# Fourier attention with routed experts: GpSimd splits the experts' weights alone, the bias is copied one mixing ahead, and batch 1's first stage begins inside batch 0

## The chip, the cores and the metric

One core of one Trainium2 chip runs the whole program. The metric is the device time of one execution in microseconds (us); of several runs the median is given. The core's compute engines run side by side, each in its own instruction order: TensorE (PE, its weight loads are listed apart as PEld), VectorE (DVE), ScalarE (ACT) and GpSimd (POOL). SyncE (SP) issues the transfers between the chip's memory and the core, in order too.

## What is computed

The reference takes 8 sequences of 2496 tokens with 256 numbers each through a Fourier mixing, and its result through a layer of 8 experts, of which each token uses one:

```python
X = np.fft.rfft(x, axis=1)
Yr = Xr @ w_r - Xi @ w_i + b_r
Yi = Xr @ w_i + Xi @ w_r + b_i
Yr = sign(Yr) * maximum(abs(Yr) - 0.01, 0);  Yi = sign(Yi) * maximum(abs(Yi) - 0.01, 0)
y = np.fft.irfft(Yr + 1j * Yi, n=2496, axis=1)

logits = y @ w_gate + modality_bias[modality_id]        # 19968 tokens, 8 experts
e_idx = argmax(logits);  gate = softmax(logits)[e_idx]
out = gate * (maximum(y @ w1[e_idx], 0) @ w2[e_idx])     # 256 -> 1024 -> 256
```

## The kernel before

**Attention.** The Fourier transform of 2496 points is done as 39 times 64 points, both stages as matrix products. Per batch `b` there are four pieces of work.

- The first stage has 11 chunks `c` (`s1_load`, `s1_split`, `s1_chunk`). A chunk's input `x` is split into a rounded part `x1h` and a rest `x1l` (L250, L251); three products (L266 to L268) go into one PSUM tile; ACT copies it into half of an `ev` buffer (L271); when an `ev` buffer is full, SP stores it to the scratch `scr` in memory (L275). There are three `ev` buffers. In batch 0 two of them are borrowed, at pair 3, for constants (`tri_st` L411 and `st_g` L206) until pair 6.
- The second stage goes over 10 pairs `p` of frequencies. `a_load` brings a pair from `scr` (L283), `s2_pair` transforms it (L292) and splits it into `Xh` and `Xl` (ACT L297 and L299, DVE L298 and L300). `mix_bias` has ACT copy the bias into a PSUM tile `mx` (L309), and `mix_sums` adds 24 products to it (L329). `shrink` makes `u` (ACT L337) and `s` (DVE L338) of it, and `is2_pair` begins the way back (L353, copied to `z` at L356). `mx` has two PSUM tiles.
- The second inverse stage has 22 pivots `j` (L369, ACT L374, DVE L375), each followed by three products into `i` (L381 to L383). Between them lie the first-stage chunks of batch `b + 2`; in batch 0 the chunks of batch 1 lie among the pairs instead.
- Routing is on DVE and GpSimd; GpSimd scatters the rows of a finished batch to their experts' places with indirect transfers (L537), four after each pair from 6 on and the rest among the pivots.

**Splitting the weights.** Through the attention, `SplitWeights` takes the experts' weights apart in 64 pieces of 128 by 512. `step` has ACT cast a loaded piece `wr` to `wh` (L978), then GpSimd or DVE subtract to get `wl` (L979); SP stores both to `wsp` (L980, L981) and loads the next piece (L963). `wh` and `wl` have one buffer each, `wr` two. The steps that lie among the pairs use GpSimd (47), those among the pivots DVE (17).

**Experts.** 78 tiles of 256 tokens (and a few half tiles) are taken through the split weights (L804 to L847).

**What sets the order.** PE, ACT, DVE and GpSimd run in an order that a scheduler fixes from the order of the code in `build`. SP issues in order too, and the number of its transfers in flight is limited, so that a transfer that has to wait holds up those behind it. `issue_after` puts transfers into SP's row behind a given one.

Of the kernel before, what the change touches and what calls it, by code (L numbers as in the profile page):

```python
# [9 lines left out]
F32 = mybir.dt.float32  # L10
# [130 lines left out]
class Attn:  # L141
# [112 lines left out]
    def s1_chunk(self, b, c, ahead):  # L254

        nc = self.nc
        u, h = c // 2, c % 2
        xh, xl = self.xs.pop((b, c))
        if h == 0:
            if u == 0 :  # L260
                self.scr[b] = self.dr.tile([2 * K1, N2P, D], F32, tag="scr", name=f"scr_{b}")
            self.ev = self.w3.tile([128, 4 * D], F32, tag="ev", name=f"ev_{b}_{u}")[:PK].rearrange("p (j d) -> p j d", d=D)

        pool, tag = (self.rps, "r") if b == 1 or c < 2 else (self.ps, "x" if b and c < 9 else "y")
        ps = pool.tile([128, 512], F32, tag=tag, name=f"s1_{b}_{c}")
        nc.tensor.matmul(ps[:PK], self.f[:, 0, :PK], xh, start=True, stop=False)  # L266
        nc.tensor.matmul(ps[:PK], self.f[:, 1, :PK], xh, start=False, stop=False)
        nc.tensor.matmul(ps[:PK], self.f[:, 0, :PK], xl, start=False, stop=True)  # L268
        if ahead and c + ahead < 11:
            self.s1_split(b, c + ahead)  # L270
        nc.scalar.copy(self.ev[:, 2 * h:2 * h + 2, :].rearrange("p j d -> p (j d)"), ps[:PK])  # L271
        if h == 1 or c == 10:
            n = min(4, J - 4 * u)
            rows = self.scr[b].rearrange("k (g j) d -> (k g) j d", g=3)
            self.stored = nc.sync.dma_start(rows[:, 4 * u:4 * u + n, :], self.ev[:, :n, :])  # L275
# [672 lines left out]
class SplitWeights:  # L948
# [17 lines left out]
            self.nc.sync.dma_start(raw.rearrange("p (c d) -> p c d", d=D), src[:, (c - 4) * 2:(c - 4) * 2 + 2, :])  # L966
        self.raw.append((e, c, raw))

    def step(self, eng):
        if not self.raw:  # L970
            return
        nc = self.nc
        e, c, raw = self.raw.pop(0)
        hi = self.one.tile([128, 512], F32R, tag="wh", name=f"wh_{e}_{c}")
        lo = self.one.tile([128, 512], F32R, tag="wl", name=f"wl_{e}_{c}")
        row = self.wsp[e * 128:(e + 1) * 128, :]
        o = c * 512 if c < 4 else 4096 + (c - 4) * 512
        nc.scalar.copy(hi, raw)  # L978
        eng.tensor_sub(lo, raw, hi)  # L979
        nc.sync.dma_start(row[:, o:o + 512], hi.bitcast(F32))  # L980
        nc.sync.dma_start(row[:, o + 2048:o + 2560], lo.bitcast(F32))  # L981
        self.load()


def build(tc, I, out, nb):
    nc = tc.nc
    with ExitStack() as outer:
        dp = outer.enter_context(tc.tile_pool(name="wsp", bufs=1, space=DRAM))
        wsp = dp.tile([E * 128, 8192], F32, name="wsp")
        with ExitStack() as ctx:  # L990
# [39 lines left out]
            at.consts_first()  # L1030
            for u, v in ((0, 1), (1, 2), (2, 5)):
                at.s1_load(0, u, v)
            ins = at.s1_load(0, 5)
            with tc.issue_after(ins.ins):
                mixing = at.consts_mix()
                next(mixing, None)
                at.table_load("m", 0)
            at.s1_split(0, 0)
            at.s1_split(0, 1)
            for c in range(11):  # L1040
                at.s1_chunk(0, c, 2)
            with tc.issue_after(at.stored.ins):
                at.s1_load(1, 0)
                ins = load(0)
            with tc.issue_after(ins.ins):
                load(1)
                at.s1_load(1, 1)
                load(2)
                at.table_load("q", 0)
                ins = at.s1_load(1, 2)  # L1050
            next(mixing, None)
            bias(0)
            at.s1_split(1, 0)
            at.s1_split(1, 1)
            at.s1_chunk(1, 0, 2)
            s2(0)
            at.s1_chunk(1, 1, 2)
            s2(1)
            mix(0)
            bias(1)  # L1060
            with tc.issue_after(ins.ins):
                ins = load(3)

# [2 lines left out]
            for b in range(nb):  # L1066
                done = b == nb - 1
                for p in range(10):
# [4 lines left out]
                    if b == 0:  # L1073
                        with tc.issue_after(ins.ins):
                            if p % 2 == 0 and p < 8:
                                at.table_load("m", p // 2 + 1)
                                at.table_load("q", p // 2 + 1)
                            ins = load(i + 4)
                        with tc.issue_after(ins.ins):
                            if p < 3:  # L1080
                                at.s1_load(1, p + 3)
                            if p == 3 or p > 4:
                                at.s1_load(2, max(p - 4, 0))
                            if p == 2:
                                sw.load()
                                sw.load()
                        s2(i + 2)
                        if p == 3:
                            late = [rt.consts(), at.consts_last()]
                        if p in (3, 6):  # L1090
                            for g in late:
                                next(g, None)
                        for c in ((2,), (3, 4), (5, 6), (7, 8), (9, 10))[p] if p < 5 else ():
                            at.s1_chunk(1, c, 2)
                    else:
                        if p > 0:
                            ins = load(i + 4) or ins
                            s2(i + 2)
                        u = {1: 0, 2: 1, 3: 2, 4: 3, 7: 4, 9: 5}.get(p)
                        if u is not None and b + 2 < nb:  # L1100
                            with tc.issue_after(ins.ins):
                                at.s1_load(b + 2, u)
                    if p < 6 if b > 0 else 2 < p < 8:
                        sw.step(nc.gpsimd)
                    if p > 5:
                        rt.scatter(4)
                    if done and 4 < p < 9:
                        bias(i + 2)
                    ending = i == last - 2
                    if ending:  # L1110
                        mix_last(i + 1, 0)
                    else:
                        mix(i + 1, 0 if apart else None)
                    if p < 9 and not (done and p > 4):
                        bias(i + 2)
                    if due:
                        state = next(routing, None)
                    at.is2_pair(b, p, ss.pop(i))
# [20 lines left out]
                for j in range(J):  # L1139
                    rt.scatter(1)  # L1140
                    pend.append((j, at.pivot(b, j)))
                    chunk = j % 2 == 1 and j != 15
                    if len(s1) > 4 and chunk:
                        at.s1_split(*s1[4])
                    if len(pend) > 2:
                        jj, r = pend.pop(0)
                        at.is1(b, jj, *r, nc.scalar.copy if done or jj % 2 else nc.vector.tensor_copy)
                    if j in (8, 18) or (b == 0 and j == 13) or (b == nb - 2 and j in (3, 13)):
                        sw.step(nc.vector)
                    if s1 and chunk:  # L1150
                        at.s1_chunk(*s1.pop(0), 0)
                    next(routing, None)
# [9 lines left out]
                    routing = chain(routing, rt.tiles_early())  # L1162
                if b == nb - 2:
                    rt.fence()
        with ExitStack() as ctx:
            ctx.enter_context(tc.manual_schedule(engines={ET.PE, ET.Activation, ET.DVE, ET.Pool}))
            ex = Experts(ctx, tc, I, out, rt, wsp)
# [36 lines left out]
```

## Time and profile before

| what | us |
|---|---|
| median of 3 runs (lowest, highest) | 1618.44 (1617.22, 1621.98) |
| the profiled execution: its own time | 1625.38 |
| its span, from the first instruction to the last | 1623.6 |
| busy in it: PE, PEld | 1529.5, 1486.9 |
| busy in it: DVE, ACT, POOL | 693.2, 655.9, 561.0 |
| first product of the experts | 709.64 |

The profile is of one execution. Busy time is what an engine spends in instructions, without the waits. A wait is named by who waited (engine, tile, line) and by what came last before it went on. "PEclk" is the share of its full clock that TensorE was granted. Rows of the DMA queue are those that SP issued; their second number is the time from one issue to the next, and not how long a transfer takes.

### The profile page before, as it was taken

What the parts mean: (1) busy time and instruction counts of PE and PEld (TensorE: products, weight loads), DVE (VectorE), ACT (ScalarE), POOL (GpSimd) and SP (SyncE); (2) the same over time, 40 slices, a digit from 0 to 9 for tenths busy, and PEclk for the clock granted to TensorE, in tenths of its full rate; (3) what the DMA queues carried; (4) which work ended last, traced back from release to release, by engine and by line L of the source; (5) the groups of instructions that cost most, each with busy time, mean ns of one, the idle gap of its engine ahead of it and who ended that gap; (6) DMA issues with size and microseconds to landing.
All of it is one profiled execution on the core that took longest, in us unless ns stands there. A gap on an engine that the chain in (4) does not pass through costs nothing. (4 is left out here: it accounts for less than half of the span.)

```text
span 1623.6 us, 34686 instructions
## 1 busy us (share of the span) xinstructions
PE 1529.5 (94%) x12459; PEld 1486.9 (92%) x12459; DVE 693.2 (43%) x1452; ACT 655.9 (40%) x1345; POOL 561.0 (35%) x548
## 2 busy tenths in 40 slices
PE   5899899989999969799999999999999999899998
PEld 3889898989898959699999999999999999899998
DVE  4455565556565536244333333333333333233332
ACT  3466665556665526242232233223322323232332
POOL 0121727272736341512552223222322222222332
PEclk7999999999999979889999999999999999999999
DMA  8777676767675635632343422752224227634541
GB/s 270 236 212 249 206 233 199 227 199 234 197 245 169 212 93 182 200 125 48 80 131 61 152 43 53 251 154 44 53 52 147 42 53 251 212 86 145 157 122 53
DMA packets 289103, 246.68 MB, mean 152 GB/s; under 512 B 207168, under 2 KB 242388, under 8 KB 285217
## 3 DMA queue, kind: packets, MB, share of 16 engines
q1 hardware_dynamic: 269937, 202.85, 43.8%
q0 software_dynamic: 18992, 41.58, 7.7%
q8 instruction: 100, 1.64, 0.4%
q14 instruction: 74, 0.61, 0.1%
HBM read 434.30 MB, written 100.73 MB: 330 GB/s over the span
## 5 line engine op out<-in xcount | busy, mean ns | idle before, releaser
L834 PE MATMUL y<-w,hh 128*128 128x256 f32 x2496 | 436.4, 278 | 0.0
L804 PE MATMUL h<-xh,w 128*128 128x256 f32 x2496 | 404.3, 279 | 5.4 <-DMA w<-wsp 5.4
L834 PEld LDWEIGHTS y<-w,hh 128*128 128x128 f32 x2496 | 378.2, 188 | 0.8
L834 PE MATMUL y<-w,hl 128*128 128x256 f32 x1248 | 347.8, 279 | 0.3 <-DVE hl L807 0.2
L804 PEld LDWEIGHTS h<-xh,w 128*128 128x128 f32 x2496 | 340.4, 189 | 5.9 <-issue 5.0
L807 DVE SCALAR_TENSOR_TENSOR hl<-h,hh 128x512 fp32r<-128x512 f32 x312 | 209.4, 689 | 234.2 <-ACT hh L806 186.5
L847 POOL DMA_INDIRECT out<-o,ix x161 | 158.4, 984 | 429.7 <-ACT o L826 392.1
L804 PE MATMUL h<-xl,w 128*128 128x256 f32 x1248 | 245.6, 278 | 0.0
L806 ACT ACTIVATE hh<-h 128x512 fp32r<-128x512 f32 x312 | 178.2, 595 | 158.1 <-PE h L804 142.2
L834 PEld LDWEIGHTS y<-w,hl 128*128 128x128 f32 x1248 | 234.2, 188 | 1.5 <-DVE hl L807 1.1
L329 PE MATMUL mx<-wmix,Xh 128*128 128x256 f32 x1280 | 188.8, 291 | 21.6 <-ACT mx L309 16.7
L329 PEld LDWEIGHTS mx<-wmix,Xh 128*128 128x128 f32 x1280 | 166.6, 195 | 29.5 <-ACT mx L309 21.3
L804 PEld LDWEIGHTS h<-xl,w 128*128 128x128 f32 x1248 | 189.8, 189 | 0.0
L826 ACT ACTIVATE o<-y,xt 128x256 f32<-128x256 f32 x78 | 37.0, 475 | 344.9 <-PE y L834 344.9
L784 POOL TENSOR_TENSOR xl<-tr,xh 128x512 fp32r<-128x512 f32 x78 | 101.0, 1295 | 210.1 <-ACT xh L783 209.3
L824 DVE TENSOR_SCALAR o<-y,xt 128x256 f32<-128x256 f32 x78 | 37.8, 484 | 316.2 <-ACT o L826 311.9
L979 POOL TENSOR_TENSOR wl<-wr,wh 128x512 fp32r<-128x512 f32 x47 | 60.0, 1277 | 277.1 <-ACT wh L978 199.0
L375 DVE TENSOR_TENSOR pl<-pv,ph 120x264 fp32r<-120x264 f32 x176 | 75.3, 431 | 100.1 <-ACT ph L374 63.3
L338 DVE SCALAR_TENSOR_TENSOR s<-mx,u 128x512 f32<-128x512 f32 (+1 forms) x81 | 55.5, 685 | 143.2 <-ACT u L337 123.7
L369 PE MATMUL pv<-pv,z 128*120 128x136 f32 x704 | 114.4, 289 | 2.1 <-ACT z L356 2.1
L369 PEld LDWEIGHTS pv<-pv,z 128*120 128x120 f32 x704 | 102.2, 191 | 9.9 <-ACT z L356 4.1
L329 PE MATMUL mx<-wmix,Xl 128*128 128x256 f32 x640 | 102.9, 284 | 1.1 <-issue 0.9
(185 smaller groups left out, 2060.1 us busy)
## 6 DMA issues: line engine op xcount, KB each, us to landing
w<-wsp SPq DMA_DIRECT2D x166, 2048.0 KB
a<-scr SPq DMA_DIRECT2D x160, 128.0 KB
xt<-xs SPq DMA_DIRECT2D x624, 32.0 KB
scr<-ev SPq DMA_DIRECT2D x40, 480.0 KB
x<-in_x SPq DMA_DIRECT2D x37, 512.0 KB
wr<-in_moe_w SPq DMA_DIRECT2D x64, 256.0 KB
wsp<-wh SPq DMA_DIRECT2D x64, 256.0 KB
wsp<-wl SPq DMA_DIRECT2D x64, 256.0 KB
```

The costliest lines, as they stand in the source:

```text
L329: self.nc.tensor.matmul(ps[i][:, i, :], t[:, 2 * i + c, o:o + 128], self.w[:, wi, c, lo, :], start=False, stop=n == len(ops) - 1, skip_gro ...
L338: nc.vector.scalar_tensor_tensor(s, ps, LAM, u, ALU.add, ALU.min)
L369: nc.tensor.matmul(ps[:PK, c * 128:c * 128 + D // 2 + E], self.z[:, o:o + 3, :, :].rearrange("p n k r -> p (n k r)"), self.pv[:, c, :], st ...
L375: nc.vector.tensor_sub(pl, ps[:PK, :GC], ph)
L784: nc.gpsimd.tensor_sub(xl, tr, xh)
L804: nc.tensor.matmul(ps[:, q, :], w1[:, lo, c, f * 128:(f + 1) * 128], x[:, c, :], start=n == 0, stop=n == 5)
L806: nc.scalar.activation(hh[:, 2 * p:2 * p + 2, :], ps, AF.Relu)
L807: nc.vector.scalar_tensor_tensor(hl[:, 2 * p:2 * p + 2, :], ps, 0.0, hh[:, 2 * p:2 * p + 2, :], ALU.max, ALU.subtract)
L824: nc.vector.tensor_scalar_mul(o[:, s, :], y[s], gate)
L834: nc.tensor.matmul(y[s], lhsT, w2[:, lo, f, :], start=n == 0, stop=n == 23)
L847: ins = self.nc.gpsimd.indirect_dma_start(out=self.out, out_offset=bass.IndirectOffsetOnAxis(ap=ix, axis=0), in_=o, in_offset=None, bounds ...
L979: eng.tensor_sub(lo, raw, hi)
```

## The change

It has three parts.

1. `step` has GpSimd do both the cast (now L982) and the subtraction (now L983), in all 64 steps. ACT loses 64 casts and DVE 17 subtractions. In batch 0 the steps lie at pairs 5 to 9 instead of 3 to 7, and the first two pieces are loaded at pair 3 instead of 2.
2. `bias(i + 2)` stands ahead of `mix(i + 1)`, so ACT copies the bias of the mixing after the next one before it makes the shrink of the next one. `bias(1)` is done before the first mixing.
3. Batch 0's chunks from 6 on write into buffers of the input pool (`wx`, four buffers) instead of `ev`. Two loads of batch 1's input (`x_1_0`, `x_1_1`) go ahead of batch 0's stores, batch 1's chunks 0 to 3 are done before the first pair, and then one chunk each at pairs 0, 1 and 2, instead of one, two and two.

The lines after L258 are shifted by 4 in the changed kernel (L268 becomes L272).

```diff
@@ s1_chunk
-            self.ev = self.w3.tile([128, 4 * D], F32, tag="ev", name=f"ev_{b}_{u}")[:PK].rearrange("p (j d) -> p j d", d=D)
+            if b == 0 and u > 2:
+                ev = self.wx.tile([128, 4, D], F32, tag="x", name=f"ev_{b}_{u}").rearrange("p j d -> p (j d)")
+            else:
+                ev = self.w3.tile([128, 4 * D], F32, tag="ev", name=f"ev_{b}_{u}")
+            self.ev = ev[:PK].rearrange("p (j d) -> p j d", d=D)
@@ SplitWeights
-    def step(self, eng):
+    def step(self):
...
-        nc.scalar.copy(hi, raw)
-        eng.tensor_sub(lo, raw, hi)
+        nc.gpsimd.tensor_copy(hi, raw)
+        nc.gpsimd.tensor_sub(lo, raw, hi)
@@ build, ahead of the pairs
-            ins = at.s1_load(0, 5)
+            at.s1_load(0, 5)
+            ins = at.s1_load(1, 0)
             with tc.issue_after(ins.ins):
                 mixing = at.consts_mix()
                 next(mixing, None)
-                at.table_load("m", 0)
+                ins = at.table_load("m", 0)
+            with tc.issue_after(ins.ins):
+                at.s1_load(1, 1)
...
             with tc.issue_after(at.stored.ins):
-                at.s1_load(1, 0)
                 ins = load(0)
             with tc.issue_after(ins.ins):
-                load(1)
-                at.s1_load(1, 1)
+                ins = load(1)
+            next(mixing, None)
+            at.s1_split(1, 0)
+            at.s1_split(1, 1)
+            for c in range(4):
+                with tc.issue_after(ins.ins):
+                    at.s1_chunk(1, c, 2 if c < 2 else 0)
+            with tc.issue_after(ins.ins):
                 load(2)
                 at.table_load("q", 0)
                 ins = at.s1_load(1, 2)
-            next(mixing, None)
             bias(0)
-            at.s1_split(1, 0)
-            at.s1_split(1, 1)
-            at.s1_chunk(1, 0, 2)
+            bias(1)
             s2(0)
-            at.s1_chunk(1, 1, 2)
             s2(1)
+            at.s1_split(1, 4)
             mix(0)
-            bias(1)
@@ build, the pairs
-                            if p == 2:
+                            if p == 3:
                                 sw.load()
                                 sw.load()
...
-                        for c in ((2,), (3, 4), (5, 6), (7, 8), (9, 10))[p] if p < 5 else ():
-                            at.s1_chunk(1, c, 2)
+                        for c in ((4,), (5,), (6,), (7, 8), (9, 10))[p] if p < 5 else ():
+                            at.s1_chunk(1, c, 1)
...
-                    if p < 6 if b > 0 else 2 < p < 8:
-                        sw.step(nc.gpsimd)
+                    if p < 6 if b > 0 else p > 4:
+                        sw.step()
                     if p > 5:
                         rt.scatter(4)
-                    if done and 4 < p < 9:
+                    if p < 9:
                         bias(i + 2)
                     ending = i == last - 2
                     if ending:
                         mix_last(i + 1, 0)
                     else:
                         mix(i + 1, 0 if apart else None)
-                    if p < 9 and not (done and p > 4):
-                        bias(i + 2)
@@ build, the pivots
-                        sw.step(nc.vector)
+                        sw.step()
```

**SP at the start, before.** The names are `c_` for constants, `x_b_u` for input of batch b (four chunk halves), `ev_b_u` for a result of the first stage and `a_p` for a pair. Here the last stores of batch 0 go out and the first pairs come in.

```order
L421 DMA mb<-in_moe_modality_bias 117x16
L275 DMA scr_137<-ev_0_138 120x1024
L275 DMA scr_137<-ev_1_158 120x1024
L275 DMA scr_137<-ev_2_178 120x1024
L275 DMA scr_137<-ev_3_198 120x1024
L275 DMA scr_137<-ev_4_218 120x1024
L275 DMA scr_137<-ev_5_234 120x512
L239 DMA x_66<-in_x 128x1024
L283 DMA a_0_242<-scr_137 64x2x256 x2
L283 DMA a_1_245<-scr_137 64x2x256 x2
L239 DMA x_66<-in_x 128x1024
L283 DMA a_2_249<-scr_137 64x2x256 x2
```

The same place in the change:

```order
L279 DMA scr_139<-ev_1_160 120x1024
L279 DMA scr_139<-ev_2_180 120x1024
L279 DMA scr_139<-ev_3_200 120x1024
L279 DMA scr_139<-ev_4_220 120x1024
L279 DMA scr_139<-ev_5_236 120x512
L287 DMA a_0_243<-scr_139 64x2x256 x2
L287 DMA a_1_246<-scr_139 64x2x256 x2
L279 DMA scr_261<-ev_0_262 120x1024
L279 DMA scr_261<-ev_1_282 120x1024
L287 DMA a_2_294<-scr_139 64x2x256 x2
```

Two loads of batch 1's input (512 KB each) have left this place and stand ahead of the stores; two stores of batch 1 have come between `a_1` and `a_2`. By the tiles' sizes SP has sent 7.27 MiB when `a_0` is in before, and 7.77 MiB in the change; when batch 1's `ev_3` is stored, 17.30 and 17.80 MiB.

**ACT in batch 0, pairs 3 and 4, before.** In brackets stands what an instruction waits for; a DMA entry is one of SP's transfers, in the two `ev` rows the store that frees the buffer.

```order
L271 COPY ev_3_513<-s_1_7_594 120x512 [waits PE_49]
L271 COPY ev_4_604<-s_1_8_605 120x512 [waits DMAHW0_49,PE_49,Activation_49]
L978 CAST wh_0_614<-wr_0_488 128x512 [waits DMAHW7_49]
L337 ACTIVATE u_4_0_646<-mx_4_551,nlam 128x512 [waits PE_49]
L309 COPY mx_5_650<-bias 128x512
L297 CAST Xh_6_668<-s_0_6_663 128x4x128 [waits PE_49]
L299 ACTIVATE Xh_6_668<-s_0_6_663 128x4x64 [waits DVE_49]
L271 COPY ev_4_604<-s_1_9_674 120x512 [waits PE_49]
L271 COPY ev_5_680<-s_1_10_681 120x512 [waits DMAHW6_49,PE_49,Activation_49]
```

The same place in the change:

```order
L275 COPY ev_3_505<-s_1_7_590 120x512 [waits PE_49]
L275 COPY ev_4_600<-s_1_8_601 120x512 [waits DMAHW2_49,PE_49,Activation_49]
L313 COPY mx_5_610<-bias 128x512
L341 ACTIVATE u_4_0_636<-mx_4_515,nlam 128x512 [waits PE_49]
L301 CAST Xh_6_656<-s_0_6_651 128x4x128 [waits PE_49]
L303 ACTIVATE Xh_6_656<-s_0_6_651 128x4x64 [waits DVE_49]
L275 COPY ev_4_600<-s_1_9_662 120x512 [waits PE_49]
L275 COPY ev_5_672<-s_1_10_673 120x512 [waits DMAHW3_49,PE_49,Activation_49]
```

The cast of `wh` is gone from ACT, and the bias of `mx_5` is copied ahead of `u_4`; the two `ev` copies still wait for a transfer.

**GpSimd in batch 1, pairs 4 to 7, before.** `x1l_c` are the rests of batch 3's chunks, the scatters (`xs`) take four rows of tokens each time, and a number behind a name only tells tiles apart.

```order
L979 TENSOR_TENSOR wl_4_1729<-wr_4_1594,wh_4_1728 128x512
L532 TENSOR_SCALAR x1b<-tok 117x22
L251 TENSOR_TENSOR x1l_0_1778<-x_0_1517,x1h_0_1777 117x512
L979 TENSOR_TENSOR wl_5_1796<-wr_5_1659,wh_5_1795 128x512
L251 TENSOR_TENSOR x1l_1_1840<-x_0_1517,x1h_1_1839 117x512
L537 DMA xs<-x1b,si_0_1710 162048x264 x4
L251 TENSOR_TENSOR x1l_2_1906<-x_1_1586,x1h_2_1905 117x512
L537 DMA xs<-x1b,si_0_1710 162048x264 x4
```

The same place in the change:

```order
L982 CAST wh_4_1728<-wr_4_1594 128x512
L983 TENSOR_TENSOR wl_4_1729<-wr_4_1594,wh_4_1728 128x512
L536 TENSOR_SCALAR x1b<-tok 117x22
L251 TENSOR_TENSOR x1l_0_1778<-x_0_1517,x1h_0_1777 117x512
L982 CAST wh_5_1795<-wr_5_1659 128x512
L983 TENSOR_TENSOR wl_5_1796<-wr_5_1659,wh_5_1795 128x512
L251 TENSOR_TENSOR x1l_1_1840<-x_0_1517,x1h_1_1839 117x512
L541 DMA xs<-x1b,si_0_1710 162048x264 x4
```

A cast stands ahead of each `wl`; what follows `wl_5` is the same row as before. In the pivots the steps 6 and 7 of each batch now stand behind the last scatters of this row.

## Rows read from the trace of the kernel before

**Rows 1.** Busy time by stretch: us, each engine (instructions), PEclk, DMA share, GB/s.

```profile
40.00:60.00 20.00, 19.91 (x154) 18.90 (x155) 13.24 (x24) 9.80 (x20) 0.00 (x0) 1.00 0.96 289
80.00:107.00 27.00, 22.99 (x185) 22.61 (x185) 12.06 (x29) 13.16 (x25) 11.04 (x11) 0.94 0.75 234
...
800.00:1200.00 400.00, 399.81 (x3449) 397.83 (x3448) 138.73 (x256) 120.40 (x220) 130.50 (x122) 1.00 0.39 101
```

**Rows 2.** Waits of PE, 0 to 107 us: total us, times, longest.

```profile
PE s L266 <- ACT ev L271: 6.8, 2, 3.8
...
PE mx L329 <- ACT mx L309: 5.7, 3, 3.5
```

**Rows 3.** Waits of ACT, 0 to 110 us.

```profile
ACT ev L271 <- DMA scr<-ev: 14.9, 3, 7.6
...
ACT wh L978 <- DMA wsp<-wh: 4.7, 1, 4.7
...
ACT wh L978 <- DMA wr<-in_moe_w: 2.9, 1, 2.9
```

**Rows 4.** Timeline of ACT's `ev` copies: start, us, instruction, [idle before, releaser].

```profile
17.44 0.58 ACT L271 COPY ev<-s 120x512 f32<-120x512 f32 x1 [3.38 <-DMA scr<-ev]
...
68.06 0.58 ACT L271 COPY ev<-s 120x512 f32<-120x512 f32 x1 [7.55 <-DMA scr<-ev]
...
76.56 0.58 ACT L271 COPY ev<-s 120x512 f32<-120x512 f32 x1 [3.99 <-DMA scr<-ev]
```

**Rows 5.** Timeline of PE, batch 0, pairs 6 to 9.

```profile
78.79 1.19 PE L329 MATMUL mx<-wmix,Xh 128*128 128x256 f32 x8 [1.74 <-ACT mx L309]
...
83.33 1.19 PE L329 MATMUL mx<-wmix,Xh 128*128 128x256 f32 x8
...
105.97 1.06 PE L353 MATMUL zs<-c_q,s 128*128 128x128 f32 x8
```

**Rows 6.** Waits of PE, 107 to 560 us (batch 0's pivots to batch 5's).

```profile
PE mx L329 <- ACT mx L309: 10.1, 11, 1.9
PE i L381 <- issue: 7.5, 6, 1.7
PE pv L369 <- ACT z L356: 1.6, 4, 0.8
PE s L268 <- POOL x1l L251: 1.2, 1, 1.2
PE i L381 <- ACT x L384: 1.0, 2, 0.6
```

**Rows 7.** Groups of instructions of the weights' split: busy, mean ns, idle before.

```profile
L979 POOL TENSOR_TENSOR wl<-wr,wh 128x512 fp32r<-128x512 f32 x47 | 60.0, 1277 | 277.1 <-ACT wh L978 199.0 <-DMA a<-scr 36.4 <-DMA wsp<-wl 19.7
...
L978 ACT CAST wh<-wr 128x512 fp32r<-128x512 f32 x64 | 39.8, 622 | 21.3 <-DMA wsp<-wh 18.0 <-DMA wr<-in_moe_w 2.9 <-DMA a<-scr 0.4
...
L979 DVE TENSOR_TENSOR wl<-wr,wh 128x512 fp32r<-128x512 f32 x17 | 11.6, 683 | 1.1 <-ACT wh L978 0.7 <-issue 0.4
```

**Rows 8.** Timeline of GpSimd, batch 2's pivots: chunk 5's rest and the last scatter.

```profile
270.87 1.28 POOL L251 TENSOR_TENSOR x1l<-x,x1h 117x512 fp32r<-117x512 f32 x1
...
279.06 0.99 POOL L537 DMA_INDIRECT xs<-x,si  x1 [0.30 <-issue]
```

**Rows 9.** Timeline of PE: the product that takes that rest.

```profile
273.56 0.39 PE L268 MATMUL s<-x1l,c_f 117*120 117x512 f32 x1
```

**Rows 10.** Waits of PE, 560 to 712 us (batches 6 and 7).

```profile
PE i L381 <- ACT x1b L384: 8.7, 2, 8.5
...
PE mx L329 <- ACT mx L309: 0.9, 1, 0.9
```

**Rows 11.** Busy time by stretch (columns as in the first group), before the experts begin.

```profile
705.00:710.00 5.00, 4.79 (x39) 4.55 (x39) 2.32 (x6) 3.75 (x12) 0.00 (x0) 1.00 0.02 3
```

**Rows 12.** Timeline of PE: the attention's last product and the experts' first.

```profile
709.52 0.29 PE L383 MATMUL i<-pl,c_g 120*117 120x264 f32 x1
709.64 0.41 PE L804 MATMUL h<-xh,w 128*128 128x256 f32 x2
```

More of the change, by code (lines that the diff above doesn't have):

```diff
@@ L1164, in build @@
                     rt.fence()
+        assert not sw.todo and not sw.raw
         with ExitStack() as ctx:
```

## The prediction

> **What bounds the kernel now.** I read the busy time by stretch first. Between 800 and 1200 us PE is busy 399.81 of 400 us at its full clock [rows 1]: the experts' phase is a matter of products alone, and the change has no line in it. The experts' first product starts where the attention's last one ends [rows 12], and in the 5 us around that the DMA share is 0.02 [rows 11], so their weights are in by 705 us at the latest and PE does not wait for them. The change can only win or lose ahead of 709.64 us, and what it saves of PE's time there comes off the end, as long as those weights come as much sooner.
>
> The second view is PE's waits, stage by stage, because there the stages differ. Up to 107 us PE waits 6.8 us for ACT's `ev` copies and 5.7 us for ACT's bias copies [rows 2]. ACT's own waits tell why: it stood 14.9 us at `ev` copies for a store of the same buffer, and 4.7 and 2.9 us at casts of `wh`, for a store and for a load [rows 3]. ACT works in order, so the bias copy behind such a cast or copy waits too. From 107 to 560 us PE waits 10.1 us in 11 places for the bias copy, and little else that has a name [rows 6]. From 560 us on the named waits are one of 8.5 us in a long run of scatters, and 0.9 us for the bias [rows 10].
>
> **Term 1, batch 0 to 107 us: -8 us.** Three places.
>
> First, the stall of 3.38 us at 17.44 us, where the first stage waits for its own store [rows 4]. In the change `ev_3` to `ev_5` of batch 0 lie in other buffers, and the order shows no such wait. Against that, 1 MiB of input goes ahead of the stores; at 289 GB/s, the rate in a stretch with a DMA share of 0.96 [rows 1], this is 3.6 us of transfer. What the first stage gains and what the transfers lose about cancel at `a_0`. Later the queue stands at 17.80 instead of 17.30 MiB when batch 1's `ev_3` is stored, 0.5 MiB or 1.8 us more, but the work behind the first wait, which feeds that queue, is 3.4 us sooner: net 1.6 us, and the wait that ends at 68.06 us [rows 4] ends some 2 us sooner. It stays, since `ev_3`, `ev_4` and `ev_5` of batch 1 still go through one buffer: -2 us.
>
> Second, the wait for the next store, ending at 76.56 us. The two `ev` copies stand 8.50 us apart [rows 4]; in the change no cast (0.62 us [rows 7]) and no store of `wh` or `wl` lies between them. I take 7.5: -1 us.
>
> Third, the rest of the pairs. From the mixing at 78.79 us to the end of the last product of this stage, 105.97 + 1.06, are 28.24 us [rows 5], at a mean clock of 0.94 [rows 1]. A pair takes 4.54 us where nothing waits, from one mixing to the next, 78.79 to 83.33 [rows 5]. Five pairs make 22.7, and I add 0.7 for the last shrink: 23.4, so 4.8 less. Those 4.8 us are the casts' waits of 4.7 and 2.9 us on ACT [rows 3], part of which the bias copies pass on. Sum: -2 - 1 - 4.8, or -8. The bounds are a loss of 3.6 us, if the extra megabyte comes through to the pairs and nothing is won, and a gain of 12.5 us, if both waits of rows 2 go.
>
> **Term 2, batch 0's pivots to batch 5: -9 us.** A bias copied one mixing ahead needs both PSUM tiles of `mx` a shrink sooner: the tile of the pair before is free when its `s` is made, long before the next mixing. ACT also loses 64 casts of 0.62 us, 39.8 us in all [rows 7], which lay between `u` and the bias. So I let the 10.1 us go, with the 1.6 us at `z` and the 1.0 us at the result copies, which ACT also made late: 12.7 us [rows 6], about 2.5 a batch.
>
> What is late next is GpSimd. In batch 2's pivots its rest `x1l` for chunk 5 ends at 270.87 + 1.28 = 272.15 us, and PE wants it at 273.56 [rows 8, 9]: 1.41 us of slack (four batches have 1.4 to 1.5, one has none and waits 1.2 us [rows 6]). Ahead of it stands an unbroken chain of scatters and rests that begins behind the step at pair 5, and that step is now a cast longer. The trace has no cast on GpSimd. Its bounds are ACT's cast of 622 ns and GpSimd's own subtraction of 1277 ns [rows 7]; below nothing is out, as the cast is an instruction that was not there. I take 0.9 us, nearer the cast, the same operation with one input less than the subtraction. Of the 2.5 us that PE gains in a batch I put 1.0 behind the chain's start. So PE asks 1.0 sooner and GpSimd is 0.9 later, 1.9 against 1.41: 0.5 us lost in four batches and 1.8 in the fifth, 3.8 in all. -12.7 + 3.8 = -9. At the bounds of the cast the term is about -10 and -7.
>
> The steps themselves cost nothing beside that. Cast and subtraction take 2.2 us against a pair's 4.54, and GpSimd was idle 277.1 us ahead of its 47 subtractions, mostly for the cast that is now its own [rows 7]. DVE loses 17 times 683 ns [rows 7], no wait of PE hung on them. In the pivots steps 6 and 7 now stand behind the last scatter, which ends at 279.06 + 0.99 [rows 8], and SP's stores of `wh` and `wl` wait for them, with the `ev` stores behind. Should that cover go, ACT's `ev` copies wait as in batch 0.
>
> **Term 3, batches 6 and 7: -2 us.** The bias wait of 0.9 us goes [rows 10], and one of two runs of scatters is broken up by two steps of the split, for which I take 1 us off. The 8.5 us wait [rows 10] stays: its scatters stay.
>
> **Sum.** -8 - 9 - 2 = -19 us. The profiled execution took 1625.38 us (span 1623.6), 0.4% more than the median of 1618.44; I take the same difference off the median: **1599.4 us**. A measurement of this kernel tells about 0.3%, 4.9 us, from no change.
>
> **The rivals.**
>
> *The opening is bound by transfers.* Between 40 and 60 us the DMA share is already 0.96 [rows 1], and 1 MiB more is ahead. If batch 0 ends as late as before, only terms 2 and 3 remain: -11, or 1607 us. For it: both long waits of ACT are for stores [rows 3]. Against: the later part, 80 to 107 us, has a share of 0.75 [rows 1].
>
> *More goes than I count.* If both waits of rows 2 go (-12.5), GpSimd's chain keeps its slack (-12.7), and half of the unnamed waits go (3.7 of 7.5 [rows 6]), with term 3 at -2, it is -31 or 1588 us. For it: PE is seldom held by anything else. Against: the `ev` waits stay in the order.
>
> *The weights' load becomes the bound.* The weights were in between the last scatters and 705 us, at least 4.6 us ahead of need [rows 11, 12]. If GpSimd's scatters of the last batch do not come sooner although PE does, the gain is cut at somewhat more than 4.6: about 1612 us. Against: scatters follow routing, which follows the products.
>
> *GpSimd becomes the bound: slower.* In each of five batches PE waits for chunk 5's rest. My sum has a cast of 0.9 us; each further us of it costs 5 us in all. The gain of 19 us is gone at 0.9 + 19/5 = 4.7 us a cast, and at 6 us the time is 1625 us. For it: the chain of scatters has no gap, and it is longer by a cast for certain. Against: a subtraction with two inputs takes 1.28 us there [rows 7], and a cast of 4.7 would need DVE or a transfer to hold GpSimd up, which none of 47 subtractions shows in its mean.
>
> The Trainium skill speaks against this part: its page "GPSIMD Engine Reference", section 4.1, sends elementwise work to VectorE, since GpSimd is about twice as slow with two inputs (with one about as fast), and section 1 says that the two engines share their interfaces. By that the 17 subtractions taken from DVE are a loss. The trace agrees on the size, 1277 against 683 ns [rows 7], but shows the engine idle ahead of them, so that the rule by itself moves no term. By section 3.1's best case of 769 ns for 512 elements the cast would be an estimated 0.77 us, and the sum -19.6.
>
> **How the numbers follow.** The forecast has a chance of 0.50, the opening bound by transfers 0.22, more than I count 0.15, the weights' load 0.06, GpSimd as the bound 0.07. The range is 1588 to 1612: it takes in the second and the third case, the bounds of term 1 with term 2 as it is, and leaves the last. Faster by over 0.3% (under 1613.6) takes the first three and a part of the fourth, less the tails: 0.86. Within 0.3%: the rest of the fourth and the edge of the last, 0.08. Slower: 0.06.
>
> **What would show it.** In the profile after, the experts' first product should start near 690 us. PE's waits for the bias copy should be gone after 107 us; the first stage of batch 0 should have no wait for a store; and ACT's two waits for `ev` stores should end near 66 and 73 us. The waits of PE for GpSimd's `x1l` should have grown from 1.2 to some 4 us. GpSimd's cast should stand between 0.62 and 1.28 us. If the last product of batch 0's pairs still ends at 107 us, term 1 is wrong; if PE waits for `x1l` 10 us or more, GpSimd is the bound; and if the bias copy is still waited for, ACT was held by something other than order.

## The result, and the profile after

The changed kernel took 1600.17 us (median of 4 runs, 1591.86 to 1601.97) against 1617.83 for the kernel before (4 runs): a ratio of 0.9875, with a 95% interval of 0.9837 to 0.9914. Two later groups of runs gave 0.9827 (0.9800 to 0.9855) and 0.9847 (0.9814 to 0.9879). The forecast was 1599.4. The total was right; its parts were less so, and that is what the experiments are about.

The two profiled executions took 1625.38 and 1600.25 us, 25.1 apart, where the medians lie 17.7 apart: the one before lies 7.5 us above its median, so that the differences in the table sum to more than the change is worth. In the table, a batch's "pairs" run from the end of the last product of the batch before (L383, L387 after) to its first pivot product (L369, L373), its "pivots" from there to its own last product; batches 6 and 7 end where the experts' first product begins.

| stretch | before, us | after, us | difference | forecast |
|---|---|---|---|---|
| start to batch 0's first pivot | 108.3 | 105.2 | -3.1 | -8 |
| pairs of batches 1 to 5 | 253.1 | 238.9 | -14.2 | -9 with the next row |
| pivots of batches 0 to 5 | 172.4 | 171.6 | -0.8 | in the row above |
| batches 6 and 7 | 175.8 | 170.7 | -5.1 | -2 |
| experts | 914.0 | 912.1 | -1.9 | 0 |

The experts' first product follows the attention's last, as it did [rows 12], 23.3 us sooner. In the timeline of PE:

```profile
686.25 0.28 PE L387 MATMUL i<-pl,c_g 120*117 120x264 f32 x1
686.37 0.40 PE L808 MATMUL h<-xh,w 128*128 128x256 f32 x2
```

**Batch 0.** PE's waits up to 107 us, which answer to [rows 2]: total, times, longest.

```profile
PE s L270 <- DVE x1h L250: 13.3, 5, 5.6
PE s L296 <- DMA a<-scr: 5.6, 1, 5.6
PE s L296 <- issue: 4.8, 1, 4.8
```

Neither the `ev` copy nor the bias copy is named any more. PE now stands 10.4 us at L296 (L292 before), once for the first pair of `scr` and once with nothing named. ACT's timeline has both waits for a store still, and both end later than before, 1.9 and 1.3 us [rows 4]:

```profile
69.92 0.59 ACT L275 COPY ev<-s 120x512 f32<-120x512 f32 x1 [6.22 <-DMA scr<-ev]
...
77.86 0.59 ACT L275 COPY ev<-s 120x512 f32<-120x512 f32 x1 [3.44 <-DMA scr<-ev]
```

The first of them still reaches PE, under another name. ACT makes its next shrink late, DVE waits for that, and DVE's cast of batch 1's input, which PE waits for, comes behind it:

```profile
71.64 0.69 DVE L342 SCALAR_TENSOR_TENSOR s<-mx,u 128x512 f32<-128x512 f32 x1 [5.84 <-ACT u L341]
```

```profile
74.88 0.59 PE L270 MATMUL s<-x1h,c_f 117*120 117x512 f32 x1 [2.79 <-DVE x1h L250]
```

After 80 us nothing is late. The busy time by stretch, against the second of [rows 1], has PE busy through:

```profile
80.00:105.00 25.00, 25.00 (x216) 24.74 (x215) 14.08 (x31) 14.47 (x27) 13.90 (x15) 1.00 0.79 245
```

**Batches 1 to 5.** PE's waits from 107 to 545 us; the bias copy of [rows 6] is gone, and other waits have come.

```profile
PE i L385 <- DVE x L388: 6.0, 3, 2.3
PE pv L373 <- ACT z L360: 3.8, 2, 2.5
PE s L272 <- POOL x1l L251: 3.4, 3, 1.2
```

That last one is the wait that the prediction named as next. GpSimd's timeline and PE's, batch 1's pivots: the rest of chunk 5 ends at 188.23 us, and PE, which has waited 1.21 us for it, goes on 0.05 us later (before, it was ready 1.41 us ahead of need in batch 2's pivots [rows 8, 9]).

```profile
186.96 1.27 POOL L251 TENSOR_TENSOR x1l<-x,x1h 117x512 fp32r<-117x512 f32 x1
```

```profile
188.28 0.49 PE L272 MATMUL s<-x1l,c_f 117*120 117x512 f32 x1 [1.21 <-POOL x1l L251]
```

The groups of the weights' split, against [rows 7]: GpSimd's cast takes 623 ns, as long as ACT's 622.

```profile
L983 POOL TENSOR_TENSOR wl<-wr,wh 128x512 fp32r<-128x512 f32 x64 | 82.6, 1291 | 49.2 <-DMA wsp<-wl 46.3 <-DMA a<-scr 0.2
...
L982 POOL CAST wh<-wr 128x512 fp32r<-128x512 f32 x64 | 39.9, 623 | 112.8 <-DMA wsp<-wh 100.4 <-issue 12.3 <-POOL x1b L536 0.2
```

### The profile page after: what moved, and what is told of

It reads as the page before. It is cut to its first block, busy times and chain, and to the rows that moved or that the text cites. A ratio compares the mean times of both kernels' runs of the same rounds, so it can differ in the third digit from the quotient of the medians.

```text
span 1598.5 us, 34701 instructions
## 1 busy us (share of the span) xinstructions
PE 1521.1 (95%) x12459; PEld 1484.9 (93%) x12459; DVE 689.7 (43%) x1435; ACT 625.2 (39%) x1281; POOL 625.1 (39%) x629
## 5 line engine op out<-in xcount | busy, mean ns | idle before, releaser
L373 PE MATMUL pv<-pv,z 128*120 128x136 f32 x704 | 115.8, 291 | 4.6 <-ACT z L360 4.3
L373 PEld LDWEIGHTS pv<-pv,z 128*120 128x120 f32 x704 | 103.2, 193 | 12.6 <-ACT z L360 5.8
L983 POOL TENSOR_TENSOR wl<-wr,wh 128x512 fp32r<-128x512 f32 x64 | 82.6, 1291 | 49.2 <-DMA wsp<-wl 46.3
```

Of the source, the lines that this page charges most:

```text
L373: nc.tensor.matmul(ps[:PK, c * 128:c * 128 + D // 2 + E], self.z[:, o:o + 3, :, :].rearrange("p n k r -> p (n k r)"), self.pv[:, c, :], st ...
L983: nc.gpsimd.tensor_sub(lo, raw, hi)
```

## The experiments

Three groups of four runs, each on a chip of its own. In the first the kernel before took 1573 us, in the others 1619.5 and 1620; so each ratio is to the kernel before in the same group, and stretches of the first group are not put beside those of the others without saying so. A stretch is read from one profile. The changed kernel, profiled on three occasions, has 102.5 to 105.8 us to the first pivot, 234.4 to 238.9 in the pairs and 171.6 to 174.6 in the pivots: single differences of 3 us say little.

### Each part alone, and a longer cast

`e1_split_only` is the kernel before with GpSimd's `step`:

```diff
-    def step(self, eng):
+    def step(self):
...
-        nc.scalar.copy(hi, raw)
-        eng.tensor_sub(lo, raw, hi)
+        nc.gpsimd.tensor_copy(hi, raw)
+        nc.gpsimd.tensor_sub(lo, raw, hi)
```

> The kernel before with part 1 alone: GpSimd casts and subtracts in all 64 steps, all else as before. Theory A (the bias copy was late because of its place behind the shrink): PE's waits for the bias copy between 107 and 560 us shrink only a little, from 10.1 us to 6 or more, and the kernel gains 3 to 7 us, half of it in the rest of batch 0's pairs, where two casts on ACT had waited 4.7 and 2.9 us. Theory B (the bias copy was late because the casts stood ahead of it on ACT): the bias waits fall under 2 us and the gain is 12 us or more. Theory C (GpSimd is the bound): no gain or slower, with PE's waits for the rest x1l at 5 us or more.

`e2_bias_only` is the kernel before with the bias ahead (ahead of the pairs, `bias(1)` moves up behind `bias(0)`):

```diff
...
-                    if done and 4 < p < 9:
+                    if p < 9:
                         bias(i + 2)
...
-                    if p < 9 and not (done and p > 4):
-                        bias(i + 2)
```

> The kernel before with part 2 alone: the bias is copied one mixing ahead, all else as before. Theory A: PE's waits for the bias copy between 107 and 560 us fall from 10.1 to under 1 us, the kernel gains 9 to 13 us, and PE's waits for x1l of chunk 5 stay near 1 to 2 us because GpSimd has no cast. Theory B: they stay above 5 us, since the casts still stand ahead on ACT, and the gain is under 5 us.

`e3_opening_only` is the changed kernel with these two edits turned back.

> The kernel before with part 3 alone: batch 0's later results in other buffers, two loads of batch 1 earlier, chunks 0 to 3 of batch 1 ahead of the pairs, and the split's first steps at pairs 5 to 9. From the trace of the changed kernel, where PE waited 10.4 us for the pairs 0 and 2 and both stalls on the store of ev ended 1.3 to 1.9 us later than before: theory A says that this part alone gains nothing, the time is between 3 us better and 4 us worse, and the pivots of batch 0 begin between 107 and 112 us (108.3 before, 105.2 with all parts). The rival, that this part brought the 3 us that batch 0 gained, has them begin near 105.

`f3_cast_x4` is the changed kernel with

```diff
-        nc.gpsimd.tensor_copy(hi, raw)
+        for _ in range(4):
+            nc.gpsimd.tensor_copy(hi, raw)
```

> The changed kernel with each cast on GpSimd written four times (the same result each time), so that a step takes 4 x 0.61 + 1.29 = 3.7 us instead of 1.9. Theory A (GpSimd's chain already sets chunk 5 in three of five batches): PE's waits for x1l grow from 3.4 us to 7 to 12, and the time grows by 4 to 9 us against the changed kernel, about 1592 x 1.0 or 1605 to 1609 us. The rival (GpSimd has room, the waits of 3.4 us are small change): the time stays within 3 us of the changed kernel's 1600.

Measured: the split alone 0.9853 (0.9829 to 0.9877), the bias ahead alone 1.0029 (1.0014 to 1.0044), the opening alone 0.9994 (0.9979 to 1.0008), the cast four times 1.1122 (1.1093 to 1.1150). The whole gain came with the split, and the bias ahead alone lost a little. PE's waits from 107 to 540 us, the split alone:

```profile
PE s L268 <- POOL x1l L251: 11.3, 5, 2.5
```

and the bias ahead alone:

```profile
PE s L268 <- POOL x1l L251: 15.1, 5, 3.7
PE mx L329 <- ACT mx L309: 5.0, 8, 1.5
```

So theory B of the first two is right in this group where it says that the casts made the bias late: without them on ACT no wait for the bias is left, though the copy stands where it stood, and with them 5.0 us remain, though the copy stands ahead. ACT's casts still wait for the store that frees `wh`, 8.9 us in nine places in the second of these runs. The misses: theory A expected 3 to 7 us from the split, which won 23, and 9 to 13 from the bias, which won nothing; theory C expected no gain if the waits for `x1l` reach 5 us, and they are 11.3. For the opening a first pivot between 107 and 112 us was expected, and it came at 104.6; the bias alone, without the opening, has it at 105.2, so that the opening need not be the cause. What the kernel before has there in this group was not profiled.

The longer cast shows how near the limit the step is. I expected 4 to 9 us. The changed kernel was not run in this group; the ratio lies 0.127 above that of the split alone, about 200 us. PE's waits from 107 to 660 us:

```profile
PE s L272 <- POOL x1l L251: 83.6, 27, 5.5
PE rk L508 <- POOL oh L495: 29.3, 5, 6.3
```

and GpSimd's there:

```profile
POOL wh L983 <- DMA wsp<-wh: 147.6, 34, 9.0
```

Per wait that is 147.6 / 34 = 4.3 us until the store of the last `wh` has landed, against 76.1 / 32 = 2.4 us in the changed kernel between 107 and 515 us:

```profile
POOL wh L982 <- DMA wsp<-wh: 76.1, 32, 5.3
```

From one cast to the next the changed kernel takes 4.7 to 7.6 us in the pairs of batches 2 and 3, the longer cast 4.8 to 12.9. That moves what follows the steps. In batch 1's timeline the first scatter of the longer cast comes with the first pivot, which is at 198.8 us; in the changed kernel's batch 2 the first scatter comes 19 us ahead of the first pivot, which is at 256.8:

```profile
198.43 1.20 POOL L541 DMA_INDIRECT xs<-x1b,si  x1 [0.21 <-issue]
```

```profile
237.43 1.08 POOL L541 DMA_INDIRECT xs<-x,si  x1 [0.18 <-issue]
```

So the scatters and rests that lay beside the pairs 6 to 9 lie in the pivots, and about three quarters of PE's waits for a rest are there. TensorE's clock adds to it. Between the profiles of the split alone and of the longer cast, 191.8 us apart, PE is idle 131 us longer, and busy 61 us longer with as many products: in batch 1's pivots it was granted 0.78 of its clock, against 0.94 in the split alone. That the one buffer of `wh` ties the step to its store I read from these rows; a second buffer was not tried. Part of the wait is SP's order: the `wh` that was cast by 236.5 us went out at 240.28, behind stores of `ev`.

### Chunk 5 without GpSimd

`g0_before` and `g1_after` are the two kernels unchanged, as a measure for the group.

> The kernel before, unchanged, profiled on the chip of this group of runs, so that the parts can be read against it. If GpSimd's chain for chunk 5 is what made the bias alone and the opening alone worthless, PE waits for x1l in each of five batches here already (2 us or more each, 10 to 15 us together, against 1.2 us in the trace read first), and for the bias copy about 10 us. If it was something else, the waits for x1l are under 5 us.

> The changed kernel, unchanged, on the chip of this group. Theory A (only the split's move pays, the bias ahead and the opening add nothing to it): its ratio to the kernel before lies within 0.005 of the 0.985 that the split alone reached, and PE's waits for x1l are 10 us or more. Theory B (the three parts add up): the ratio is 0.975 or less.

`h1_split_chunk5` (from the split alone) and `f2_chunk5_dve` (from the changed kernel) have one more edit, which gives the rest of chunk 5 to DVE in batches 2 to 7:

```diff
-        (nc.gpsimd if b > 1 and c < 6 else nc.vector).tensor_sub(xl, x, xh)
+        (nc.gpsimd if b > 1 and c < 5 else nc.vector).tensor_sub(xl, x, xh)
```

> The kernel before with the split on GpSimd, and the rest x1l of chunk 5 made by DVE, which already makes those of chunks 6 to 10, so that GpSimd's chain is one subtraction shorter and PE's product for chunk 5 no longer hangs on it. Theory A (GpSimd's chain is the bound that is left in the batches): PE's waits for x1l fall from 11.3 us to under 2 and the time by 7 to 11 us against the split alone, a ratio of 0.978 to 0.981 to the kernel before. The rival (another engine is as late there): the waits for x1l go, but waits of about the same sum for DVE or ACT take their place and the ratio stays at 0.984 or above.

> The changed kernel with the rest x1l of chunk 5 made by DVE. Theory A: 7 to 12 us faster than the changed kernel, and now the bias ahead shows, if it is worth anything: a ratio below that of the split alone with the same edit. The rival: no gain, waits for DVE in place of those for GpSimd.

The kernel before has 3.9 us of waits for `x1l` between 107 and 540 us and 10.0 for the bias copy, so chunk 5 alone does not make the bias ahead worthless in this group; and the changed kernel has 5.0, half of what theory A wanted.

Measured: the changed kernel 0.9827 (0.9800 to 0.9855), the split with chunk 5 on DVE 0.9964 (0.9945 to 0.9983), the changed kernel with it 0.9929 (0.9903 to 0.9955). I had expected a gain of 7 to 12 us and got a loss of 17 (1608.75 against 1591.05). The waits for `x1l` went, which the changed kernel has in this group:

```profile
PE s L272 <- POOL x1l L251: 5.0, 5, 1.2
PE i L385 <- DVE x L388: 3.3, 3, 2.2
PE i L385 <- DVE x1b L388: 3.1, 3, 1.8
```

but in the changed kernel with chunk 5 on DVE others make 18.1 us, where the last two lines here make 6.4 (both from 107 us to the end of batch 5):

```profile
PE i L385 <- issue: 6.1, 4, 2.6
PE i L385 <- DVE x1b L388: 6.0, 2, 3.1
PE i L385 <- DVE x L388: 6.0, 2, 3.3
```

One of them in the timelines, batch 1's pivots. GpSimd no longer has a subtraction between its scatters; ten run on end, from 183.28 to 196.51:

```profile
194.21 1.00 POOL L541 DMA_INDIRECT xs<-x1b,si  x1 [0.30 <-issue]
195.51 1.00 POOL L541 DMA_INDIRECT xs<-x1b,si  x1 [0.31 <-issue]
```

and near their end PE and ACT stand together, with nothing that names the cause:

```profile
197.73 0.53 PE L385 MATMUL i<-ph,c_g 120*117 120x264 f32 x1 [2.58 <-issue]
```

```profile
197.90 0.38 ACT L378 CAST ph<-pv 120x264 fp32r<-120x264 f32 x1 [1.11 <-remote]
```

The pivots of batches 0 to 5 take 187.5 us with this edit and 172.4 without. Of these 15.1 us PE is idle 8.6, and busy 6.6 longer with as many products: the granted clock there is 0.95, against 0.99. (The profiles also differ by 4.6 us up to the first pivot, where the edit changes nothing.) The rival is right that others are late there, but DVE's own work is not shown to be why. My reading, that longer runs of scatters hold all engines up, fits the place; it was not tried by itself.

### The parts side by side on one chip

`k1_after` is the changed kernel, `k2_split_only` is `e1_split_only` again, and `k3_split_undone` and `k4_bias_undone` are the changed kernel with one part turned back:

```diff
# k3_split_undone
-    def step(self):
+    def step(self, eng):
...
-        nc.gpsimd.tensor_copy(hi, raw)
-        nc.gpsimd.tensor_sub(lo, raw, hi)
+        nc.scalar.copy(hi, raw)
+        eng.tensor_sub(lo, raw, hi)
# k4_bias_undone
-                    if p < 9:
+                    if done and 4 < p < 9:
                         bias(i + 2)
...
+                    if p < 9 and not (done and p > 4):
+                        bias(i + 2)
...
```

> The changed kernel again, unchanged, as the measure for the three runs beside it on the same chip. Its ratio to the kernel before was 0.9875 and 0.9827 on two occasions; expected 0.980 to 0.988.

> Part 1 alone again (GpSimd splits, all else as before), now beside the changed kernel on one chip. Theory A (the split carries the gain, the other parts are worth nothing): within 0.004 of the changed kernel's ratio. Theory B (the bias ahead is worth something once the casts are off ACT): 0.006 or more above the changed kernel's.

> The changed kernel with part 1 undone: ACT casts, GpSimd subtracts among the pairs and DVE among the pivots; the bias ahead and the opening stay. Theory A: no gain is left, a ratio of 0.996 to 1.006, and PE still waits for the bias copy, 4 us or more, since casts that wait for a transfer stand ahead of it on ACT. Theory B (the bias ahead wins by itself): a ratio of 0.993 or less, with the bias waits under 1 us.

> The changed kernel with part 2 undone: the bias is copied behind the shrink, as before; GpSimd splits and the opening stays. Theory A: within 0.003 of the changed kernel's ratio, with PE's waits for the bias copy between 107 and 540 us at 2 us or less. Theory B: 0.005 or more above it, with those waits at 6 us or more.

Measured, with the stretches of the table above in the profiled execution; the first line is `g0_before`, of the second group and so of another chip, where the kernel before takes nearly as long (1619.5 and 1620.1 us). The profiled executions of the split alone and of the version without the bias are the slowest of their six, 4.0 and 3.6 us above the median.

| kernel | ratio (interval) | to first pivot | pairs 1 to 5 | pivots 0 to 5 | batches 6, 7 |
|---|---|---|---|---|---|
| before | 1 | 107.5 | 251.1 | 174.9 | 173.2 |
| all three parts | 0.9847 (0.9814 to 0.9879) | 105.8 | 236.8 | 174.6 | 168.0 |
| split alone | 0.9876 (0.9849 to 0.9904) | 101.7 | 245.1 | 167.5 | 174.8 |
| bias and opening, no split | 1.0013 (0.9990 to 1.0036) | 105.1 | 242.6 | 187.6 | 175.1 |
| split and opening, no bias | 0.9870 (0.9843 to 0.9898) | 103.2 | 245.5 | 172.0 | 169.1 |

The ratios are theory A's: the split carries nearly all of the gain, and without it none is left. What the other two add to it, 0.003, is within the intervals. Only the waits for the bias with the bias turned back, 5.5 us, are nearer theory B's 6 than theory A's 2. The columns say why. The bias ahead does what it should among the pairs, 245.5 to 236.8 with the split, and 251.1 to 242.6 without it (here the opening, too, is in, which moves no work of these pairs). But in the pivots it is given back: without the split 174.9 becomes 187.6. With the split it is 172.0 and 174.6, and that lies within what the changed kernel's own profiles differ by.

PE's timelines split the pairs further, by the time from one mixing's first product to the next one's. Of the nine such intervals in a batch's pairs, the steps of the weights' split lie among the first seven and none in the last two. The sums are over batches 1 to 5, in us.

| kernel (group) | first seven | last two |
|---|---|---|
| before (second) | 173.4 | 51.9 |
| all three parts (third) | 161.9 | 46.5 |
| split alone (third) | 161.9 | 54.8 |
| bias and opening, no split (third) | 171.8 | 46.0 |
| split and opening, no bias (third) | 162.1 | 54.8 |
| split alone (first) | 162.1 | 46.2 |
| bias ahead alone (first) | 170.8 | 46.0 |
| opening alone (first) | 174.8 | 45.8 |

So each part has its own place. The split wins some 10 us where the casts stood on ACT, with and without the bias ahead. The bias ahead wins 6 to 8 us in the last two intervals, where no cast stands, and only in the later groups: there, with the split alone, ACT begins the shrink ahead of the last mixing 1.9 us after the last sum that it takes, in all five batches, and the bias copy comes behind it. From the split alone of the third group, batch 1 (PE's last sum, then ACT):

```profile
167.22 0.62 PE L329 MATMUL mx<-wmix,Xl 128*128 128x256 f32 x4
```

```profile
169.81 0.69 ACT L337 ACTIVATE u<-mx,nlam 128x512 f32<-128x512 f32 x1 [2.85 <-PE s L292]
```

The same kernel in the first group, 0.1 us after the sum, so that the bias ahead had nothing to win there:

```profile
165.65 0.64 PE L329 MATMUL mx<-wmix,Xl 128*128 128x256 f32 x4
```

```profile
166.38 0.69 ACT L337 ACTIVATE u<-mx,nlam 128x512 f32<-128x512 f32 x1 [1.16 <-PE mx L329]
```

What holds ACT up there no row names; GpSimd is in its run of scatters in both.

PE's waits from 105 to 540 us, pairs and pivots, of the kernel without the split:

```profile
PE s L272 <- POOL x1l L251: 8.8, 5, 3.5
PE i L385 <- DVE x L388: 7.3, 4, 2.3
PE mx L333 <- ACT mx L313: 4.8, 6, 2.2
PE i L385 <- DVE x1b L388: 3.5, 3, 1.8
```

In all five batches PE waits for chunk 5's rest, once each (3.9 us in three places before). What is left of the bias waits has the cast ahead of it, which waited for a store, in ACT's timeline of this kernel:

```profile
224.55 0.62 ACT L982 CAST wh<-wr 128x512 fp32r<-128x512 f32 x1 [0.66 <-DMA wsp<-wh]
225.07 0.58 ACT L313 COPY mx<-bias 128x512 f32<-128x512 f32 x1
```

The split alone has the shortest pivots, 167.5 us. ACT has no cast and DVE no subtraction there; which of the two it is was not tried. PE still waits for the bias, from 101 to 540 us, once a batch, at the last mixing:

```profile
PE mx L329 <- ACT mx L309: 6.3, 5, 1.4
PE i L381 <- issue: 3.5, 3, 1.7
```

With the split in, the opening costs rather than gains: the first pivot comes at 100.0 to 101.7 us in the three profiles of the split without it, and at 101.2 to 107.1 in the six with it. No version tried beats the changed kernel beyond its interval.

## Why the prediction was right, and where it was wrong

**What bounds the kernel: right.** The experts' phase hardly moved (914.0 to 912.1 us), and what PE saved ahead of it came off the end, with the experts' start still on PE.

**Term 1, -8 us: the mechanism half right, the sum too large.** Measured are -3.1, and -5.0 and -1.7 in the later groups (102.5 and 105.8 against 107.5). The third step, -4.8 us for the pairs 6 to 9, was right and low: the 28.24 us [rows 5] became 22.24 (81.73 to 103.97 us), 6.0 less, and the split alone brings the first pivot 5.8 us forward (101.7 against 107.5). The first step, -2, had the wrong sign: the first of the two waits for `ev` stores ended 1.9 us later, at 69.92 and not near 66. The second, -1, was right and too large: the two copies stand 7.94 us apart instead of 8.50, so that the second wait ended 1.3 us later. What failed in the first step is that the work which feeds SP's stores would run 3.4 us sooner. The extra transfers did come through: PE's first product for a pair begins at 30.37 us, 30.18 before, so that the chunks done ahead of it are paid for by the wait of 5.6 us, and pair 1's mixing at 45.08 instead of 41.75, behind the wait of 4.8 us; the load of `a_2` now stands behind two stores. So the first rival, the opening bound by transfers, holds for pairs 0 to 5; it does not for 6 to 9, where the casts had been in the way.

**Term 2, -9 us: right in sign, and low.** Measured are -15.0, and -19.2 and -14.6 in the later groups. That the bias waits go was right. The prediction let them go for the copy's new place and for the casts together. By the intervals, taking the casts off is worth some 10 us in the pairs and the new place 6 to 8, but without the split the place wins nothing in the end (1.0029 alone, 1.0013 with the opening). That GpSimd's rest for chunk 5 is late next was right, and so was its size: the waits grew from 1.2 to 3.4 us (5.0 and 4.8 in the later groups), forecast were some 4. Two steps failed. The gain in the pairs was summed from PE's waits, 10.1 us, and it is 14.2: a mixing that waits for nothing begins before the product ahead of it ends (83.33 us [rows 5], against 82.52 + 1.06 = 83.58), and a wait counts only from that end, so that each late mixing loses some 0.25 us more than its wait shows. And the split was costed at nothing in the pivots: "no wait of PE hung on" DVE's subtractions. By single profiles the split alone takes 5 to 7 us off them (167.5 against 172.4 and 174.9), and the waits for the copies of `i` on DVE and ACT fall from 8.6 us to 3.2 (107 to 540 us, `g0_before` and `k2_split_only`). Against this, the 1.6 and 1.0 us of waits for `z` and for these copies, which the sum let go, are 3.8 and 6.6 us in the profile after.

**Term 3, -2 us: low.** Batches 6 and 7 took 5.1 us less. In the later groups they took 168.0, 169.1 and 167.9 us in kernels with split and opening, 173.2 before and 174.8 with the split alone; which edit it is was not settled.

**The cast.** I took 0.9 us, between 0.62 and 1.28; it took 0.623, the lower end. The rival "GpSimd becomes the bound" was priced at 5 us for each microsecond more. The longer cast, 2.64 - 0.62 = 2.0 us more, cost about 200, where this price gives 10: it took the wait for one rest a batch as all that a later GpSimd brings, and not that the whole run of scatters and rests then falls into the pivots. Its point of decision lay far nearer than the 4.7 us I gave. The rule in the Trainium skill that I weighed against the split, "GPSIMD Engine Reference", section 4.1, has GpSimd about twice as slow with two inputs, and the trace agrees (1291 ns against VectorE's 683); with one input it has GpSimd roughly at line rate, and here GpSimd takes 623 ns for a cast of 128x512 and VectorE 418 (L199). The rule did not decide the time, because the split relieved the two engines that PE waits for. By the best case in section 3.1 of that page of the Trainium skill the cast would be an estimated 0.77 us; the trace has 0.62, and the measurement decides.

So the total, 0.05% from the median, was right in part by luck: a term too large (1) and two too small (2 and 3) cancel in part. In the profiles read first the three make -23.2 us and not -19, and the profile before lies 7.5 us above its median, the one after on it. From `g0_before` to `k1_after` they make -21.5, and the experts take 2.2 us longer.

## What to carry to other kernels

Ask of an in-order engine what stands ahead of a late instruction and waits for a transfer. Moving the late one forward and taking the waiting one off that engine are two remedies for two causes, and only the gain taken place by place shows which of them wins where. Sum a gain from the intervals of the loop and not from the waits alone. When a stage gets faster, follow the chain that runs beside it (here the rests and scatters on GpSimd) through the next stage, because there the gain can be given back; and a step on that chain is cheap only as long as the chain ends with its stage.

## What the runs showed that was not expected

The first group of runs was 2.9% faster as a whole. In the profile of the split alone batches 6 and 7 took 134.3 us there and 174.8 us in the third group, the experts 910.7 and 916.4. In the first group PE had no wait without a releaser above 0.2 us in these batches, while GpSimd ran eight scatters on end (548.83 to 558.91 us); in the others such waits are up to 8.1 us long in these batches. ACT's late shrink, above, is the same in kind: one kernel, late in one group and not in the other. That the runs of scatters cause them is not shown, nor what differs between the groups, except that each had a chip of its own.
